# A windowed attention and ReGLU kernel: order of the first loads, weights 4 to 7 in one request, inverse sums ahead of the outputs

## The chip, the cores and the metric

One core of a Trainium2 chip. The time is device microseconds of one execution, with medians of several runs; the kernel before takes 266.7 us. A run counts as slow when it is over 1.5% above the fastest of its kernel. Two runs told here do, one of four in each of two experiments, which say so; the medians include them, the ratios don't. Kernels of different rounds are compared by their ratios. By the 2% mark that the prediction uses, a ratio between 0.98 and 1.02 would be called the same; where such a ratio is called a gain or a loss here, its interval leaves out 1. A ratio is the mean time of one kernel's fast runs over that of the other's of the same rounds, with a 95% interval, so it is not quite the ratio of the medians quoted beside it. A profile is of one execution and counts from its first instruction; its span is about 2 us shorter than the time.

## The reference, cut to what matters

```python
B, H, S, D = 4, 8, 768, 64                  # q, k, v: float32
scores = (q @ k.T) / 8                      # per head
keep   = (key < 4) | (0 <= query - key < 128)
a      = softmax(where(keep, scores, -1e9))
x      = concat_heads(a @ v)                # [3072, 512]
out    = (relu(x @ w_gate) * (x @ w_val)) @ w_out     # d_ff = 1536
```

Only a band of 128 keys and four sink keys counts. The work is cut in units of a batch and a pair of heads (four pairs a batch), and each unit in two parts of 384 queries. The FFN of a batch has two parts of 12 slots: a slot is 128 of the 1,536 columns, so it needs all four pairs' outputs of its part and one slice of each of the gate and value weights ("weights 0" to "weights 11").

## The kernel before

A static program: instructions are recorded in a fixed order, each engine runs its own in that order. Scores go through an exponential into `ee`. An output (called V below: V01 is pair 0, part 1) is two groups of matmuls, then work on DVE:

```python
PP = [pspool.tile([128, 2, 512], F32, name=f"pp{i}") for i in range(2)]   # two banks in each tile
G  = [pspool.tile([128, 512], F32, name=f"g{i}") for i in range(4)]       # one bank in each tile

def two():
    if head[0]:                              # the first 20 us
        srot[0] += 2
        return G[srot[0] % 4][:], G[(srot[0] + 1) % 4][:]
    x = pair()                               # the next of the two PP tiles
    return x[:, 0, :], x[:, 1, :]

def V(u, part, between=None):
    pv, pd = two()
    ...
    sums(pd, lambda j, h: ones[:])           # PE: row sums of ee
    if between: between()
    sums(pv, lambda j, h: vn[u.b % 2][:, j, 2 * u.p + h, :])   # PE: ee times V
    ...
    nc.vector.transpose(out=t1[:], in_=pd[:, 0:CUT])           # DVE: inverse of the row sums
    nc.vector.reciprocal(r[:], ...)
    nc.vector.transpose(out=R[:]..., in_=r[:]...)
    nc.vector.tensor_tensor(xT[...], pv[:, 0:CUT], R[:], op=Alu.mult)
```

There are 32 such outputs: four in the head (part 0 of the first batch), 28 among the FFN slots. V01 to V31 of the first batch follow slots 6 to 9. Loads in float32, nearly all on SP's queue: k and q of the first batch in eight halves, V in blocks j. Weights are requested by POOL, which casts them to bf16 on the way. POOL also casts most of k, q and V, in program order. A "gate" is a tiny write into a load's target that keeps SP from issuing the load before the program has come that far.

```python
# head, cut: loads and the requests of weights
for c in (6, 7):
    gate_half(c)                             # POOL
    load_half(c)
load_w(2, 4)
T_half(4); V(U[3], 0)
load_w(4, 6)
...
# what POOL and SP do ahead of an FFN slot
prep[0] += [("half", 6), ("lv0",), ("w", 6, 8), ("half", 7), ("w", 8, 10)]   # lv0: gate (POOL) and load of V, j 3 to 6
prep[2] += [("v", 0, j) for j in (3, 4, 5, 6)]                               # casts of V
prep[3] += [("w", 10, 12)]
prep[7] += [("load", 4), ("load", 5), ("load", 6), ("lv", 1)]                # next batch
```

The softmax here doesn't subtract the row's maximum and nothing guards it: scores larger than these inputs give would overflow.

Of the kernel before, what the change touches and what calls it, by code (L numbers as in the profile page):

```python
# [19 lines left out]
def kernel(  # L20
# [12 lines left out]
    nc = tc.nc  # L33
    B, H, S, D = q.shape
    assert (B, H, S, D) == (4, 8, 768, 64)
    NP = H // 2
# [46 lines left out]
           3: (1, 0, 152, [(252, 244, 0, 140), (380, 372, 140, 152)]),  # L83
           4: (1, 152, 507, [(252, 384, 152, 267), (380, 384, 267, 507)])}

    V2 = [(4, 2, 0, 255, 112), (5, 2, 255, 399, 240), (6, 2, 399, 419, 364)]
    VSEG = [[(0, 0, 0, 247, 0), (1, 0, 247, 499, 120), (2, 1, 0, 140, 244), (3, 1, 255, 267, 372)],
            [(2, 1, 140, 255, 0), (3, 1, 267, 507, 0)] + V2]
    VSEG0 = [[(0, 0, 0, 247, 0), (1, 0, 247, 499, 120), (2, 1, 0, 140, 244), (3, 1, 140, 152, 372)],
             [(2, 1, 152, 267, 0), (3, 1, 267, 507, 0)] + V2]  # L90

    class Unit:
        def __init__(self, i):
# [18 lines left out]
    def cast_half(c, copies=(nc.gpsimd.tensor_copy, nc.gpsimd.tensor_copy)):  # L112
        for src, dst, copy in ((kf, kn, copies[0]), (qf, qn, copies[1])):
            copy(half(dst, c).rearrange("p (n h d) -> p h n d", n=3, h=2),
                                  half(src, c).rearrange("p (h n d) -> p h n d", n=3, h=2))
# [16 lines left out]
    def cast_v(b, j, rows=128, copy=nc.gpsimd.tensor_copy):  # L132
        flat = lambda ap: ap.rearrange("p h d -> p (h d)")
        copy(flat(vn[b % 2][0:rows, j, :, :]), flat(vf[0:rows, j, :, :]))  # L134
# [86 lines left out]
    def two():  # L221
        if head[0]:
            srot[0] += 2
            return G[srot[0] % 4][:], G[(srot[0] + 1) % 4][:]
        x = pair()
        return x[:, 0, :], x[:, 1, :]

    def spin(n, bank=0):

        for _ in range(n):  # L230
            nc.tensor.matmul(out=G[bank][:], lhsT=idle[:, 0:128], rhs=idle[:], start=True, stop=True)
# [18 lines left out]

    def T_half(c):
        t, x = c % NP, c // NP
        if c <= NP:
            both = pair()
            tk, tq = both[:, 0, :], both[:, 1, :]
        else:
            tk, tq = G[3][:, 0:256], G[3][:, 256:512]
        for src, ps in ((kn, tk), (qn, tq)):
            for n in range(3):
                nc.tensor.transpose(ps.bitcast(BF16)[:, 128 * n:128 * n + 128], half(src, c)[:, 128 * n:128 * n + 128],  # L260
                                    ident[:])
        vk, vq = (ps.bitcast(BF16)[:, 0:HALF].rearrange("d (n p) -> d p n", p=128) for ps in (tk, tq))
        e = kE[t]

        for r0, r1, c0 in ((0, 40, 0), (40, 124, 128), (124, 128, 384)) if x == 0 else ((0, 80, 396), (80, 128, 640)):
            nc.scalar.copy(e[:, c0:c0 + 3 * (r1 - r0)].rearrange("d (p n) -> d p n", n=3), vk[:, r0:r1])
        (nc.scalar.copy if c in (2, 3, 4) else nc.vector.tensor_copy)(
            qT[t][:, x * HALF:x * HALF + HALF].rearrange("d (p n) -> d p n", n=3), vq)
        if x == 0:
            sinks(U[t], nc.scalar.copy)  # L270
# [20 lines left out]

    ready = {}

    def V(u, part, between=None):
        pv, pd = two()
        segs = (VSEG if u.b else VSEG0)[part]

        def sums(out, w):
            for i, (j, g, c0, c1, o0) in enumerate(segs):
                for h in range(2):  # L300
                    nc.tensor.matmul(out=out[64 * h:64 * h + 64, o0:o0 + c1 - c0], lhsT=w(j, h),  # L301
                                     rhs=ee[u.i % NE][:, g, h, c0:c1], start=i == 0, stop=i == len(segs) - 1,
                                     skip_group_check=True)

        sums(pd, lambda j, h: ones[:])
        if between:
            between()
        sums(pv, lambda j, h: vn[u.b % 2][:, j, 2 * u.p + h, :])
        t1 = npool.tile([128, CUT], F32, name="t1")
        R = npool.tile([128, CUT], F32, name="R")  # L310
        r = npool.tile([128, CUT // 32], F32, name="r")
        nc.vector.transpose(out=t1[:], in_=pd[:, 0:CUT])  # L312
        nc.vector.reciprocal(r[:], t1[:].rearrange("p (c e) -> p c e", e=32)[:, :, 0])
        nc.vector.transpose(out=R[:].rearrange("p (c e) -> p c e", e=32),  # L314
                            in_=r[:].unsqueeze(2).to_broadcast([128, CUT // 32, 32]))
        nc.vector.tensor_tensor(xT[u.b % 2][:, u.p, CUT * part:CUT * part + CUT], pv[:, 0:CUT], R[:], op=Alu.mult)  # L316
        ready[u.b, u.p, part] = True

    gvn = [0]

# [34 lines left out]
    with tc.manual_schedule():  # L355
# [11 lines left out]
        setup()  # L367
        cast_half(0)
        T_half(0)
        spin(5)  # L370
        cast_half(1)
        T_half(1)
        setup2()
        Sg(U[0], 0)
        Sg(U[0], 3)
        cast_v(0, 0)
        spin(2)
        Sg(U[1], 0)
        cast_v(0, 3, 16, nc.vector.tensor_copy)
        cast_half(2)  # L380
        cast_v(0, 1)
        cast_v(0, 2)
        Sg(U[1], 3)
        V(U[0], 0, lambda: T_half(2))
        cast_half(3, (nc.gpsimd.tensor_copy, nc.scalar.copy))
        Sg(U[2], 0)
        load_w(0, 2)
        V(U[1], 0)
        Sg(U[2], 3)
        T_half(3)  # L390
        cast_half(4)
# [1 line left out]
        Sg(U[3], 0)  # L393
        cast_half(5)
        Sg(U[3], 3)
        for c in (6, 7):
            gate_half(c)
            load_half(c)
        load_w(2, 4)
        T_half(4)  # L400
        V(U[3], 0)
        load_w(4, 6)
        Sg(U[0], 4)
        T_half(5)
        Sg(U[0], 2)
        spin(3, 2)
        head[0] = False


# [8 lines left out]
            at[st] = s  # L418
            plan[s].append(st)

        for s, w in {0: "S14 S12", 2: "H2", 3: "S24 S22 H3", 5: "S34 S32", 6: "V01", 7: "V11", 8: "V21",
                     9: "V31"}.items():
            for y in w.split():
                put(s, y, 0)
        for s, w in {11: "T0", 12: "T1", 13: "S00 S01", 14: "S10 S11", 15: "T2", 16: "S20 S21", 17: "V00", 18: "V10",
                     19: "T3", 20: "V20", 21: "S30 S31", 22: "V30 S02"}.items():
            for y in w.split():
                put(s, y, 1)
        for b in range(2, B + 1):
# [5 lines left out]
            for x, y in enumerate(w.split()):  # L435
                put(24 * (b - 1) + x // 2 * 2, y[0] + y[2:], b - (y[1] == "p"))
        prep = [[] for _ in slots]
        prep[0] += [("half", 6), ("lv0",), ("w", 6, 8), ("half", 7), ("w", 8, 10)]
        prep[2] += [("v", 0, j) for j in (3, 4, 5, 6)]
        prep[3] += [("w", 10, 12)]  # L440
        prep[7] += [("load", 4), ("load", 5), ("load", 6), ("lv", 1)]
        prep[9] += [("kq", 4)]
        prep[10] += [("load", 7), ("kq", 5)]
        prep[13] += [("kq", 6)]
        prep[14] += [("v", 1, j) for j in range(7)]
        prep[16] += [("kq", 7), ("td", 8), ("wo",)]
        for i in range(ND, len(U)):
            t = at["S", i - NP, 2] + 1
# [12 lines left out]
        for s, (b, g, m) in enumerate(slots):  # L461
            for x in prep[s]:
                if x[0] == "kq":
                    cast_kq(U[x[1]])
                elif x[0] == "load":
                    gate(U[x[1]])
                    load_kq(U[x[1]])
                elif x[0] == "half":
                    cast_half(x[1])
                elif x[0] == "w":  # L470
                    load_w(*x[1:])
                elif x[0] == "wo":
                    for c in range(3):
                        load_wo(c)
                elif x[0] == "td":
                    to_dram(U[x[1]])
                elif x[0] == "turn":
                    turn(U[x[1]])
                elif x[0] == "sinks":
                    sinks(U[x[1]], nc.gpsimd.tensor_copy)  # L480
                elif x[0] == "lv0":
                    for j in (3, 4, 5, 6):
                        nc.gpsimd.memset(vf[32:33, j, 0, 0:2], 0.0)
                        load_v(0, j, 16 if j == 3 else 0)
                elif x[0] == "lv":
                    for j in range(7):
                        load_v(x[1], j)
                else:
                    cast_v(*x[1:])
            chunk(b, g, m)  # L490
            for what, i, x in plan[s]:
                if what == "T":
                    T(U[i])
                elif what == "H":
                    T_half(NP + i)
                elif what == "S":
                    Sg(U[i], x)
                else:
                    V(U[i], x)
            for _ in range(3):  # L500
                if f2:
                    f2.popleft()()
            if s == 23:
                f2 += [lambda t=t, mm=mm: ffn2(0, t, mm) for t in range(6) for mm in range(FM)]
            if b > 0 and m == FM - 1:
                f2 += [lambda b=b, t=t, mm=mm: ffn2(b, t, mm) for t in range(3 * g, 3 * g + 3) for mm in range(FM)]
# [38 lines left out]
```

## Time and profile before

| | before |
|---|---|
| time, median | 266.7 us |
| span of the profiled run, mean granted PE clock | 264.3 us, 0.986 |
| PE busy, idle | 249.9 us, 14.4 us |
| FFN slot 0, slot 7, slot 24 start | 20.5, 39.2, 78.2 us |

The first lines to read are those that the prediction shows: PE is busy 95% of the span, its one large hole is at V01, and that hole is a wait for V. In a timeline: start, duration, engine, line, operation, in square brackets the idle time before it and what ended it. Here is what an output looks like where nothing disturbs it, in the timeline of PE and DVE of the kernel before (start, duration, engine, line, operation, in square brackets the idle time before it and what ended it):

```profile
95.07 0.53 PE L301 MATMUL pp<-ee,ones 128*64 128x115 bf16 x10
95.46 0.51 PE L301 MATMUL pp<-ee,vn 128*64 128x115 bf16 x10
95.90 0.39 PE L282 MATMUL pp<-qT,kE 64*128 64x247 bf16 x4
96.02 0.58 DVE L312 STREAM_TRANSPOSE t<-pp 128x384 f32<-128x384 f32 x1 [0.21 <-PE pp L301]
```

Both groups of sums follow each other without a gap, 95.07 to 95.90 = 0.83 us, and DVE's transpose starts after the second.

### The profile page before, as it was taken

How to read it: one execution, taken by the hardware profiler on the slowest of the kernel's cores; microseconds unless marked ns; L12 is line 12 of the kernel's file. 1: busy time of each engine (PE TensorE's matmuls, PEld its weight loads, DVE VectorE, ACT ScalarE, POOL GpSimd, SP SyncE). 2: the span in 40 equal slices, each digit the busy share in tenths (PEclk: the TensorE clock that was granted, in tenths of full speed). 3: DMA queues.
4: the chain of work that ended last, by engine and by line, in shares of the span. 5: the costliest groups of instructions: out<-in, count | busy, mean ns of one | idle time of the engine just before them, and what ended most of it. 6: DMA issues, size and time to landing. Idle time of an engine off the chain costs nothing.

```text
span 264.3 us, 5502 instructions
## 1 busy us (share of the span) xinstructions
PE 249.9 (95%) x2145; PEld 140.6 (53%) x2145; DVE 149.1 (56%) x314; ACT 117.4 (44%) x226; POOL 74.0 (28%) x106
## 2 busy tenths in 40 slices
PE   7889939998989999999999999999999999999994
PEld 3465515655646555555555555555555655555441
DVE  5577718777986774666537667657355642322000
ACT  3777802386353535553434355464344233332211
POOL 6687135299920014694000044000000000000000
PEclk9999968999999999999999999999999999999999
DMA  7999999939999259499412395310110111001232
GB/s 191 255 192 215 189 300 278 190 120 71 191 169 140 56 134 198 97 166 160 93 46 62 61 218 112 93 40 2 40 42 0 42 40 41 28 16 40 79 122 79
DMA packets 81266, 30.45 MB, mean 115 GB/s; under 512 B 65368, under 2 KB 77144, under 8 KB 81240
## 3 DMA queue, kind: packets, MB, share of 16 engines
q1 hardware_dynamic: 47944, 21.83, 33.3%
q0 software_dynamic: 32752, 7.87, 31.8%
q8 instruction: 17, 0.28, 0.5%
q10 hardware_dynamic: 544, 0.39, 0.5%
q14 instruction: 9, 0.07, 0.1%
HBM read 28.48 MB, written 9.44 MB: 143 GB/s over the span
## 4 chain that ended last, share of the span: by engine, by line
PE 77%; DMA 9%; DVE 4%; POOL 3%; issue 2%; SPq 2%; ACT 2%; ACTq 0%; POOLq 0%; DVEq 0%
PE g L348 21%; PE g L328 21%; PE g L333 20%; PE pp L301 7%; DMA vf<-in_v_dram 6%; PE pp L348 4%; PE pp L282 4%; DMA qf<-in_q_dram 4%; SPq L130 2%; DVE hT L335 1%; PE pp L240 1%; POOL vn L134 1%; DVE qT L248 1%; ACT ee L286 1%; DVE R L314 1%
## 5 line engine op out<-in xcount | busy, mean ns | idle before, releaser
L335 DVE TENSOR_TENSOR hT<-gs,g 128x384 bf16<-128x384 f32 x96 | 52.9, 551 | 64.9 <-PE g L333 63.1
L331 ACT ACTIVATE gs<-g 128x384 f32<-128x384 f32 x96 | 47.4, 494 | 76.9 <-PE g L328 75.7
L333 PE MATMUL g<-xT,wv 128*128 128x384 bf16 x384 | 78.8, 328 | 1.0 <-ACT ee L286 0.6
L328 PE MATMUL g<-xT,wg 128*128 128x384 bf16 x384 | 79.0, 328 | 0.0
L348 PE MATMUL g<-wo,hT 128*128 128x512 bf16 x240 | 64.1, 380 | 0.0
L286 ACT ACTIVATE ee<-pp 128x998 bf16<-128x998 f32 (+4 forms) x52 | 45.7, 903 | 31.3 <-PE pp L282 31.0
L328 PEld LDWEIGHTS <-wg 128*128 128x128 bf16 x384 | 36.1, 98 | 31.7 <-issue 1.2
L333 PEld LDWEIGHTS <-wv 128*128 128x128 bf16 x384 | 37.5, 98 | 27.1 <-DMA wv<-in_moe_w_val_dram 2.1
L348 PEld LDWEIGHTS <-hT 128*128 128x128 bf16 x288 | 26.2, 98 | 26.2 <-issue 2.1
L289 DVE TENSOR_TENSOR ee<-ee,msk 128x838 bf16<-128x838 bf16 (+4 forms) x48 | 29.3, 619 | 8.8 <-ACT ee L286 8.6
L134 POOL CAST vn<-vf 128x512 bf16<-128x512 f32 x28 | 17.8, 653 | 39.6 <-DMA vf<-in_v_dram 39.6
L151 POOL DMA_DIRECT2D qd<-in_q_dram x8 | 25.1, 4248 | 0.0
L151 POOL DMA_DIRECT2D kd<-in_k_dram x8 | 22.7, 3676 | 0.3 <-issue 0.3
L312 DVE STREAM_TRANSPOSE t<-pp 128x384 f32<-128x384 f32 x28 | 16.3, 581 | 8.9 <-PE pp L301 8.3
L352 ACT COPY ot<-g 128x512 f32<-128x512 f32 x20 | 11.7, 585 | 18.2 <-PE g L348 17.4
L282 PE MATMUL pp<-qT,kE 64*128 64x255 bf16 (+6 forms) x240 | 17.4, 246 | 2.0 <-DVE qT L248 1.0
L314 DVE STREAM_TRANSPOSE R<-r 128x384 f32<-128x384 f32 x32 | 18.5, 578 | 1.1
L301 PE MATMUL pp<-ee,vn 128*64 128x115 bf16 (+8 forms) x256 | 14.5, 236 | 4.2 <-POOL vn L134 4.2
L301 PEld LDWEIGHTS <-ones 128*64 128x64 bf16 x288 | 12.3, 110 | 9.7 <-issue 9.4
L316 DVE TENSOR_TENSOR xT<-pp,R 128x384 bf16<-128x384 f32 x28 | 15.6, 557 | 1.0
L301 PEld LDWEIGHTS <-vn 128*64 128x64 bf16 x288 | 12.5, 111 | 5.5 <-POOL vn L134 5.4
L301 PE MATMUL pp<-ee,ones 128*64 128x115 bf16 (+8 forms) x256 | 14.5, 239 | 0.1
(76 smaller groups left out, 126.7 us busy)
## 6 DMA issues: line engine op xcount, KB each, us to landing
out_dram<-ot SPq DMA_DIRECT2D x24, 256.0 KB
vf<-in_v_dram SPq DMA_DIRECT2D x12, 256.0 KB
vf<-in_v_dram SPq DMA_DIRECT2D x12, 224.0 KB
kf<-in_k_dram SPq DMA_DIRECT2D x8, 192.0 KB
wg<-in_moe_w_gate_dram POOLq DMA_DIRECT2D x6, 256.0 KB, 7.2
wv<-in_moe_w_val_dram POOLq DMA_DIRECT2D x6, 256.0 KB, 8.9
kf<-in_k_dram SPq DMA_DIRECT2D x4, 384.0 KB
qf<-in_q_dram SPq DMA_DIRECT2D x4, 384.0 KB
```

What stands on the lines that cost most here:

```text
L134: copy(flat(vn[b % 2][0:rows, j, :, :]), flat(vf[0:rows, j, :, :]))
L151: nc.gpsimd.dma_start(out=dst[u.i - ND].rearrange("s (h d) -> s h d", h=2), in_=x[u.b, 2 * u.p:2 * u.p + 2].rearrange("h s d -> s h d"))
L282: nc.tensor.matmul(out=ps[:, h, c0:c1], lhsT=kE[t][64 * h:64 * h + 64, x0:x0 + 128], rhs=qT[t][64 * h:64 * h + 64, q0:q0 + c1 - c0], start ...
L286: nc.scalar.activation(x, ps[:, :, b0:n], Act.Exp, bias=0.0, scale=scale)
L289: nc.vector.tensor_tensor(x, x, msk[:, g, m0:m0 + c1 - c0].unsqueeze(1).to_broadcast([128, 2, c1 - c0]), op=Alu.mult)
L301: nc.tensor.matmul(out=out[64 * h:64 * h + 64, o0:o0 + c1 - c0], lhsT=w(j, h), rhs=ee[u.i % NE][:, g, h, c0:c1], start=i == 0, stop=i == l ...
L314: nc.vector.transpose(out=R[:].rearrange("p (c e) -> p c e", e=32), in_=r[:].unsqueeze(2).to_broadcast([128, CUT // 32, 32]))
L328: nc.tensor.matmul(out=gp[:, 0:CUT], lhsT=wg[:, ko, m * 128:(m + 1) * 128], rhs=x[:, ko, c], start=ko == 0, stop=ko == KO - 1)
L331: nc.scalar.activation(gs[:], gp[:, 0:CUT], Act.Relu, bias=0.0, scale=1.0)
L333: nc.tensor.matmul(out=vp[:, 0:CUT], lhsT=wv[:, ko, m * 128:(m + 1) * 128], rhs=x[:, ko, c], start=ko == 0, stop=ko == KO - 1)
L335: nc.vector.tensor_tensor(h[:, m, c], gs[:], vp[:, 0:CUT], op=Alu.mult)
L348: nc.tensor.matmul(out=op, lhsT=hT[b % 2][:, m, t * 128:(t + 1) * 128], rhs=wo[:, m, :], start=m == 0, stop=m == FM - 1)
```

## The change

The intent: bring the loads of the first phase into PE's order of use, save a request, and start DVE's inverse sums of pairs 0 and 1 before PE forms their V sums. The diff, cut to its core (a rename of one table and the later slot for the casts of the next batch's V are left out):

```diff
 def T_half(c):
-        if c <= NP:
+        if c < 2:
+            tk, tq = two()
+        elif c <= NP:

-    def V(u, part, between=None):
-        pv, pd = two()
-        ...
-        sums(pd, lambda j, h: ones[:])
-        if between:
-            between()
-        sums(pv, lambda j, h: vn[u.b % 2][:, j, 2 * u.p + h, :])
+    def V1(u, part):
+        pv, pd = two()
+        sums(u, part, pd, lambda j, h: ones[:])
         t1 = ...; R = ...; r = ...
         nc.vector.transpose(out=t1[:], in_=pd[:, 0:CUT])
         nc.vector.reciprocal(...)
         nc.vector.transpose(out=R[:]...)
+        return u, part, pv, R
+
+    def V2(u, part, pv, R):
+        sums(u, part, pv, lambda j, h: vn[u.b % 2][:, j, 2 * u.p + h, :])
         nc.vector.tensor_tensor(xT[...], pv[:, 0:CUT], R[:], op=Alu.mult)
+
+    def V(u, part):
+        V2(*V1(u, part))

 # head: V1 of pairs 0 and 1 early, V2 of both later; V(U[3], 0) ahead of T_half(4); fewer spins
+        load_w(2, 4)
         for c in (6, 7):
             gate_half(c)
             load_half(c)
-        load_w(2, 4)
 ...
-        load_w(4, 6)
+        load_w(4, 8)

-        {0: "S14 S12", 2: "H2", 3: "S24 S22 H3", 5: "S34 S32", 6: "V01", ...}
+        {0: "S14 S12", 1: "H2", 2: "S24 S22 H3", 3: "S34 S32", 6: "V01", ...}
-        {11: "T0", 12: "T1", 13: "S00 S01", ..., 18: "V10", 19: "T3", ...}
+        {12: "T0", 13: "T1", 14: "S00 S01", ..., 19: "V10 T3", ...}
-        prep[0] += [("half", 6), ("lv0",), ("w", 6, 8), ("half", 7), ("w", 8, 10)]
-        prep[2] += [("v", 0, j) for j in (3, 4, 5, 6)]
-        prep[3] += [("w", 10, 12)]
-        prep[7] += [("load", 4), ("load", 5), ("load", 6), ("lv", 1)]
+        prep[0] += [("half", 6), ("half", 7), ("w", 8, 10), ("w", 10, 12)]
+        prep[3] += [("lv0",)]
+        prep[4] += [("v", 0, j) for j in (3, 4, 5, 6)]
+        prep[8] += [("load", 4), ("load", 5), ("load", 6), ("lv", 1)]
                 # in lv0
-                        nc.gpsimd.memset(vf[32:33, j, 0, 0:2], 0.0)
+                        nc.scalar.copy(vf[32:33, j, 0, 0:2], warm[32:33, :])
```

More of the change, by code (lines that the diff above doesn't have):

```diff
@@ L84 @@
            4: (1, 152, 507, [(252, 384, 152, 267), (380, 384, 267, 507)])}
-    V2 = [(4, 2, 0, 255, 112), (5, 2, 255, 399, 240), (6, 2, 399, 419, 364)]
+    VLAST = [(4, 2, 0, 255, 112), (5, 2, 255, 399, 240), (6, 2, 399, 419, 364)]
     VSEG = [[(0, 0, 0, 247, 0), (1, 0, 247, 499, 120), (2, 1, 0, 140, 244), (3, 1, 255, 267, 372)],
-            [(2, 1, 140, 255, 0), (3, 1, 267, 507, 0)] + V2]
+            [(2, 1, 140, 255, 0), (3, 1, 267, 507, 0)] + VLAST]
     VSEG0 = [[(0, 0, 0, 247, 0), (1, 0, 247, 499, 120), (2, 1, 0, 140, 244), (3, 1, 140, 152, 372)],
-             [(2, 1, 152, 267, 0), (3, 1, 267, 507, 0)] + V2]
+             [(2, 1, 152, 267, 0), (3, 1, 267, 507, 0)] + VLAST]
     class Unit:
@@ L292, with sums @@
     ready = {}
-    def V(u, part, between=None):
-        pv, pd = two()
-        segs = (VSEG if u.b else VSEG0)[part]
-        def sums(out, w):
-            for i, (j, g, c0, c1, o0) in enumerate(segs):
-                for h in range(2):
-                    nc.tensor.matmul(out=out[64 * h:64 * h + 64, o0:o0 + c1 - c0], lhsT=w(j, h),
-                                     rhs=ee[u.i % NE][:, g, h, c0:c1], start=i == 0, stop=i == len(segs) - 1,
-                                     skip_group_check=True)
-        sums(pd, lambda j, h: ones[:])
-        if between:
-            between()
-        sums(pv, lambda j, h: vn[u.b % 2][:, j, 2 * u.p + h, :])
+    def sums(u, part, out, w):
+        segs = (VSEG if u.b else VSEG0)[part]
+        for i, (j, g, c0, c1, o0) in enumerate(segs):
+            for h in range(2):
+                nc.tensor.matmul(out=out[64 * h:64 * h + 64, o0:o0 + c1 - c0], lhsT=w(j, h),
+                                 rhs=ee[u.i % NE][:, g, h, c0:c1], start=i == 0, stop=i == len(segs) - 1,
+                                 skip_group_check=True)
+    def V1(u, part):
+        pv, pd = two()
+        sums(u, part, pd, lambda j, h: ones[:])
         t1 = npool.tile([128, CUT], F32, name="t1")
@@ L369 @@
         T_half(0)
-        spin(5)
-        cast_half(1)
-        T_half(1)
+        spin(4, 1)
         setup2()
@@ L375 @@
         Sg(U[0], 3)
+        cast_half(1)
+        T_half(1)
         cast_v(0, 0)
-        spin(2)
+        cast_v(0, 3, 16, nc.vector.tensor_copy)
+        v0 = V1(U[0], 0)
         Sg(U[1], 0)
-        cast_v(0, 3, 16, nc.vector.tensor_copy)
         cast_half(2)
@@ L383 @@
         Sg(U[1], 3)
-        V(U[0], 0, lambda: T_half(2))
+        T_half(2)
+        v1 = V1(U[1], 0)
+        V2(*v0)
+        V2(*v1)
         cast_half(3, (nc.gpsimd.tensor_copy, nc.scalar.copy))
@@ L387 @@
         load_w(0, 2)
-        V(U[1], 0)
         Sg(U[2], 3)
@@ L398 @@
             load_half(c)
-        load_w(2, 4)
+        V(U[3], 0)
         T_half(4)
-        V(U[3], 0)
-        load_w(4, 6)
+        load_w(4, 8)
         Sg(U[0], 4)
@@ L405 @@
         Sg(U[0], 2)
-        spin(3, 2)
+        spin(2, 2)
         head[0] = False
@@ L419, in put @@
             plan[s].append(st)
-        for s, w in {0: "S14 S12", 2: "H2", 3: "S24 S22 H3", 5: "S34 S32", 6: "V01", 7: "V11", 8: "V21",
+        for s, w in {0: "S14 S12", 1: "H2", 2: "S24 S22 H3", 3: "S34 S32", 6: "V01", 7: "V11", 8: "V21",
                      9: "V31"}.items():
@@ L424 @@
                 put(s, y, 0)
-        for s, w in {11: "T0", 12: "T1", 13: "S00 S01", 14: "S10 S11", 15: "T2", 16: "S20 S21", 17: "V00", 18: "V10",
-                     19: "T3", 20: "V20", 21: "S30 S31", 22: "V30 S02"}.items():
+        for s, w in {12: "T0", 13: "T1", 14: "S00 S01", 15: "S10 S11", 16: "T2", 17: "S20 S21", 18: "V00",
+                     19: "V10 T3", 20: "V20", 21: "S30 S31", 22: "V30 S02"}.items():
             for y in w.split():
@@ L444 @@
         prep[13] += [("kq", 6)]
-        prep[14] += [("v", 1, j) for j in range(7)]
+        prep[15] += [("v", 1, j) for j in range(7)]
         prep[16] += [("kq", 7), ("td", 8), ("wo",)]
```

## The prediction

> **What bounds the kernel now.** I read the page first (busy shares, the chain of waits), then the PE timeline of the first 70 us with the idle time in front of each group, then POOL's timeline and the DMA queues by stretch, because a change of load order can only act where PE waits for a load.
>
> ```profile
> PE 249.9 (95%) x2145; PEld 140.6 (53%) x2145; DVE 149.1 (56%) x314; ACT 117.4 (44%) x226; POOL 74.0 (28%) x106
> PE 77%; DMA 9%; DVE 4%; POOL 3%; issue 2%; SPq 2%; ACT 2%; ACTq 0%; POOLq 0%; DVEq 0%
> ```
>
> PE is busy for 249.9 of 264.3 us, so all its idle time is 14.4 us, and the 9% of DMA in the chain is the part that a load order could touch. The page names it: loads of V and q. From 77 us on the chain is PE alone; what is won or lost before that is carried to the end unchanged. The timeline of PE shows where the one large hole lies:
>
> ```profile
> 33.72 0.33 PE L301 MATMUL pp<-ee,vn 128*64 128x115 bf16 x4
> 35.43 0.43 PE L301 MATMUL pp<-ee,vn 128*64 128x255 bf16 x2 [1.39 <-POOL vn L134]
> 38.45 0.33 PE L301 MATMUL pp<-ee,vn 128*64 128x144 bf16 x2 [2.59 <-POOL vn L134]
> 39.01 0.23 PE L301 MATMUL pp<-ee,vn 128*64 128x20 bf16 x2 [0.23 <-POOL vn L134]
> 39.17 1.46 PE L328 MATMUL g<-xT,wg 128*128 128x384 bf16 x4
> 42.76 0.82 PE L328 MATMUL g<-xT,wg 128*128 128x384 bf16 x4
> ```
>
> This is the second half of pair 0's output sum (V01, placed after FFN slot 6): 1.39 + 2.59 + 0.23 = 4.2 us of waiting for casts of V. The next slot then runs at half clock: it takes 39.17 to 41.84 = 2.67 us, where slot 8 takes 42.76 to 44.16 = 1.40 us; 1.3 us more. So this hole is worth about 5.5 us. POOL's casts wait in turn for the V loads:
>
> ```profile
> 30.59 0.61 POOL L134 CAST vn<-vf 128x512 bf16<-128x512 f32 x1 [3.92 <-DMA vf<-in_v_dram]
> 34.76 0.61 POOL L134 CAST vn<-vf 128x512 bf16<-128x512 f32 x1 [3.56 <-DMA vf<-in_v_dram]
> 37.78 1.17 POOL L134 CAST vn<-vf 128x512 bf16<-128x512 f32 x2 [2.41 <-DMA vf<-in_v_dram]
> ```
>
> SP issued these loads from 22.44 us, and the last landed at 37.7. Why 15 us? The stretches (time, then busy time of PE, PEld, DVE, ACT, POOL, clock, DMA share, GB/s) and the queues between 30 and 34 us answer:
>
> ```profile
> 24.00:26.00 2.00, 1.70 (x15) 0.99 (x14) 1.19 (x3) 0.70 (x3) 2.00 (x4) 1.00 1.45 200
> 26.00:30.00 4.00, 4.00 (x37) 2.46 (x36) 2.88 (x7) 3.35 (x8) 0.67 (x1) 1.00 1.35 200
> 30.00:34.00 4.00, 3.37 (x37) 1.71 (x35) 2.87 (x7) 2.63 (x7) 0.61 (x1) 1.00 1.35 183
> q0 software_dynamic: 993, 0.49, 89.4%
> q1 hardware_dynamic: 956, 0.24, 45.4%
> ```
>
> The DMA engines are full (share above 1), and weights (q0, packets of 512 B) and V (q1, 256 B) go through one for one: 993 packets against 956. V therefore gets only 0.24 MB of the 0.73 MB moved in 4 us. What sets the end of the stall is the sum of all that is queued before or beside V.
>
> **What the Trainium skill says.** "DMA: Bandwidth & Descriptors", section "Queues, rings and completion order", has each DMA engine take turns between the queue rows it has work for, packet by packet; the 993 to 956 above agrees. The same page, "Issuing engines are not separate DMA queues", says that loads issued from different engines end on the same 16 engines; the trace agrees, as V does not move faster for being on SP's queue. "TensorE: Matmul & The Clock Gate", section "The HAM clock gate", says that an idle window of about 3.4 us halves the PE clock; the trace agrees: granted clock 0.50 between 36 and 42 us, 2.67 us against 1.40 us. "Perfetto Trace Analysis", section "DMA Optimizations", says that larger transfers use the bandwidth better; here I doubt that it pays: the output weights come in rows of 1,024 B and move at 199 GB/s (68 to 70 us), rows of 512 B at 200 GB/s (24 to 26 us).
>
> **The change part by part.**
>
> *1. Loads.* Before, POOL requests weights 0-1 at 12.3 us, opens the gate of the last k/q halves at 15.8, requests 2-3 and 4-5 by 18.8, opens the gate of V at 22.4, requests 6-7 at 22.4 and 8-9 at 25.2; 10-11 only after the casts of V, at 38.9. After, 2-3 come ahead of the gate (k/q about 1.5 us later), 4-7 follow in one pair of requests of twice the size, then the casts of the last halves, then 8-9 and 10-11. The gate of V moves from POOL, slot 0, to ACT, slot 3, behind the copies of the last half: those need that half's load (landed about 24 us, now about 25.5), two casts of 0.5 and a transpose with copies of about 1 us, so V is requested at about 27.5 instead of 22.4 us.
>
> Now the sum. DMA is full from 12 us until V has landed, in both kernels: the weights 4-11 cover the stretch until V starts. In front of or beside V the new order has one more pair of requests, weights 10-11: 2 x 256 KB = 0.52 MB, at 200 GB/s 2.6 us. V (224 + 256 + 256 + 40 = 776 KB) is served one for one, so it is still the last to finish. Against it: less time is shared. At 183 GB/s shared, 122 of weights and 61 of V, I estimate 12% loss against each alone (weights 200; V alone about 240). V shares about 10 us now, about 6 then: 0.5 us back. Last V landing: 37.7 + 2.6 - 0.5 = 39.8 us. Then, as now, two casts (1.2 us) and the last sums (0.4 us): slot 7 starts at about 41.3, not 39.2 us. That is +2.1 us. The stall begins a little earlier or later, but that does not matter: its end is set by the load.
>
> *2. Head.* Two separate banks for the first transposes let DVE copy q while ACT copies k: the copy at 5.99 waited for ACT, some 0.6 us. The first scores come that much sooner, two fewer filler matmuls with a larger gap follow, and sums and inverses of pairs 0 and 1 (transposes of 0.58, reciprocal 0.23, 0.58) leave before their outputs need V. Pair 3's output comes before the transposes of half 4, which then delay the first FFN slot. I estimate slot 0 at 20.2 to 21.2 us against 20.5. Whatever the sign, nothing of it reaches the end: PE then waits for V anyway. Net 0.
>
> *3. Slots.* Half 2's transposes and the scores S24 to S32 come one or two slots earlier; same work, all before V01. Net 0. They may remove the 0.30 and 0.63 us waits ahead of slot 6, hidden by the same wait.
>
> *4. Second batch one slot later* (T0 11 to 12 and so on). The spacing stays, so its waits of 0.35 (55 us), 0.67 (62 us) and 0.73 us (74 us) mostly stay; perhaps 0.5 us goes, as V10 and T3 share a slot now. Its k/q loads are gated on ACT behind slot 7's activation, so at about 43 instead of 33 us; 2.3 MB at 400 GB/s take 6 us, landing by 50, and the transposes want them from 53. It fits.
>
> Sum: +2.1 - 0.5 = +1.6 us, 266.74 to about 268.3 us.
>
> **The rivals.** (a) *The change works as named*: with weights 4-7 through earlier and fewer shared rounds, V lands sooner and the 5.5 us hole closes. This would give 261 to 264 us. Against it: V is asked for 5 us later, with 0.52 MB more ahead and full engines. (b) *SP's issue becomes the bound.* V's 256 B packets on a free queue are not always quick: 113 GB/s at DMA share 0.50 between 48 and 50 us, while SP is issuing V of the next batch. If V's tail runs at that rate rather than 240, its last 0.45 MB takes 4 instead of 1.9 us: 270 to 271 us. (c) *A new wait later*: k/q, V and output weights of the next batch all start later behind a later V; if they miss their slots at 53, 66 and 83 us, each costs one or two us: 270 to 273 us. For it: POOL is busy 20.3 of the 24 us from 54 to 78. (d) *The head sets it*: only if V landed before 33 us.
>
> **Range and chances.** V's extra wait can be 0.5 (packets well overlapped) to 4 us (rival b), the later gain 0 to 1.5: 80% from 265.3 to 270.8 us. Faster by 2% (below 261.4) needs nearly the whole hole gone: 0.05. Slower by 2% (above 272.1) needs rivals b and c together: 0.09. Within: 0.86.
>
> **What would show it.** Right: casts of V ending at 40 to 42 us with the wait on the V load; V01's wait longer than 4.2 us, near 6 to 8; slot 7 again at half clock; weight requests 8-11 all issued before 30 us; PE from slot 8 on as before, shifted by about 2 us. Step 2 right: the q copy of the first half at about 5.4, and slot 0 near 20.5 with no effect at slot 7. Wrong: V landed by 36 us, a V01 wait below 4 us, or new waits of PE between 50 and 80 us; a slot order that reaches V01 later would also prove my "net 0" false.

## The result

| | before | after |
|---|---|---|
| time, median | 266.67 us | 302.46 us |
| ratio, 95% interval | | 1.134 (1.129 to 1.139) |
| span, mean granted PE clock | 264.3 us, 0.986 | 301.1 us, 0.971 |
| PE busy, idle | 249.9, 14.4 us | 257.7, 43.4 us |
| FFN slot 0, slot 7 start | 20.5, 39.2 us | 23.0, 44.5 us |

The kernel is 36 us slower, not 1.6. At slot 7 it is only 5.4 us behind, so most of the loss comes later, where the prediction saw nothing but PE at full work. Busy engines and the chain of waits of the changed kernel:

```profile
PE 257.7 (86%) x2116; PEld 145.9 (48%) x2141; DVE 153.0 (51%) x314; ACT 118.0 (39%) x230; POOL 71.3 (24%) x100
PE 72%; DVE 10%; DMA 7%; ACT 3%; issue 3%; POOL 2%; SPq 0%; DVEq 0%; POOLq 0%; ACTq 0%
```

DVE has gone from 4% to 10% of the chain although it has the same 314 instructions. (Of PE's 29 missing instructions, four are filler matmuls that the change leaves out; 25 are records that the trace lost, which makes PE's idle time look about 1 us too long.) The list of who waited for whom (total us, how often, the longest) names it. These are the lines of PE among the sums:

```profile
PE pp L300 <- DVE t L311: 24.8, 28, 1.9
PE pp L300 <- POOL vn L134: 5.8, 4, 4.1
```

The first line does not exist in the kernel before. In each of the 28 outputs outside the head PE now waits for DVE's transpose between its two groups of sums. One of them, from the timeline of the changed kernel, to be held against the four lines shown of before:

```profile
92.34 0.53 PE L300 MATMUL pp<-ee,ones 128*64 128x115 bf16 x10
92.99 0.58 DVE L311 STREAM_TRANSPOSE t<-pp 128x384 f32<-128x384 f32 x1
93.60 0.23 DVE L312 RECIPROCAL r<-t 128x12 f32<-128x12 f32 x1
93.62 0.54 PE L300 MATMUL pp<-ee,vn 128*64 128x115 bf16 x10 [0.74 <-DVE t L311]
94.09 0.36 PE L284 MATMUL pp<-qT,kE 64*128 64x255 bf16 x6
```

The transpose reads the row sums between 92.99 and 93.57, and the V sums start 0.05 us after it has ended, though they need nothing of it. From the first sum to the next work PE takes 94.09 - 92.34 = 1.75 us in place of 0.83.

The other part of the loss is there too, at V01. Timelines of PE and POOL of the changed kernel, for the lines of before that the prediction shows:

```profile
37.30 0.24 PE L300 MATMUL pp<-ee,vn 128*64 128x115 bf16 x2 [0.74 <-DVE t L311]
38.66 0.29 PE L300 MATMUL pp<-ee,vn 128*64 128x240 bf16 x2 [1.12 <-POOL vn L134]
43.03 0.43 PE L300 MATMUL pp<-ee,vn 128*64 128x255 bf16 x2 [4.08 <-POOL vn L134]
44.54 1.46 PE L334 MATMUL g<-xT,wg 128*128 128x384 bf16 x4
...
37.99 0.61 POOL L134 CAST vn<-vf 128x512 bf16<-128x512 f32 x1 [5.14 <-DMA vf<-in_v_dram]
43.16 1.17 POOL L134 CAST vn<-vf 128x512 bf16<-128x512 f32 x2 [0.18 <-DMA vf<-in_v_dram]
```

V's last casts end at 44.3 us; before it was 38.95, and I had predicted 40 to 42.

### The profile page after: what moved, and what is told of

It reads as the page before. It is cut to its first block, busy times and chain, and to the rows that moved or that the text cites. A ratio compares the mean times of both kernels' runs of the same rounds, so it can differ in the third digit from the quotient of the medians.

```text
span 301.1 us, 5493 instructions
## 1 busy us (share of the span) xinstructions
PE 257.7 (86%) x2116; PEld 145.9 (48%) x2141; DVE 153.0 (51%) x314; ACT 118.0 (39%) x230; POOL 71.3 (24%) x100
## 4 chain that ended last, share of the span: by engine, by line
PE 72%; DVE 10%; DMA 7%; ACT 3%; issue 3%; POOL 2%; SPq 0%; DVEq 0%; POOLq 0%; ACTq 0%
PE g L334 20%; PE g L339 19%; PE g L354 18%; PE pp L300 5%; DVE t L311 5%; DVE hT L341 4%; PE pp L284 4%; DMA qf<-in_q_dram 4%; PE pp L354 3%; DMA vf<-in_v_dram 3%; ACT ee L288 2%; PE pp L240 1%; DMA kf<-in_k_dram 1%; DVE qT L248 1%; PE g L231 1%
## 5 line engine op out<-in xcount | busy, mean ns | idle before, releaser
L334 PE MATMUL g<-xT,wg 128*128 128x384 bf16 x384 | 80.8, 334 | 0.4 <-DVE qT L269 0.2
L339 PE MATMUL g<-xT,wv 128*128 128x384 bf16 x384 | 79.7, 331 | 0.0
L354 PE MATMUL g<-wo,hT 128*128 128x512 bf16 x217 | 61.5, 386 | 1.3 <-issue 0.3
L334 PEld LDWEIGHTS <-wg 128*128 128x128 bf16 x384 | 36.8, 100 | 33.3 <-issue 3.8
L339 PEld LDWEIGHTS <-wv 128*128 128x128 bf16 x384 | 38.2, 100 | 26.1 <-issue 2.0
L300 PE MATMUL pp<-ee,vn 128*64 128x115 bf16 (+8 forms) x256 | 15.4, 239 | 30.6 <-DVE t L311 24.8
L300 PEld LDWEIGHTS <-vn 128*64 128x64 bf16 x288 | 15.6, 110 | 33.3 <-issue 26.7
L134 POOL CAST vn<-vf 128x512 bf16<-128x512 f32 x28 | 16.8, 617 | 39.8 <-DMA vf<-in_v_dram 39.8
L284 PE MATMUL pp<-qT,kE 64*128 64x255 bf16 (+6 forms) x240 | 17.5, 249 | 2.0 <-ACT qT L269 1.0
L300 PEld LDWEIGHTS <-ones 128*64 128x64 bf16 x288 | 12.8, 111 | 11.3 <-issue 10.7
```

The costliest lines, as they stand in the source:

```text
L284: nc.tensor.matmul(out=ps[:, h, c0:c1], lhsT=kE[t][64 * h:64 * h + 64, x0:x0 + 128], rhs=qT[t][64 * h:64 * h + 64, q0:q0 + c1 - c0], start ...
L300: nc.tensor.matmul(out=out[64 * h:64 * h + 64, o0:o0 + c1 - c0], lhsT=w(j, h), rhs=ee[u.i % NE][:, g, h, c0:c1], start=i == 0, stop=i == l ...
L334: nc.tensor.matmul(out=gp[:, 0:CUT], lhsT=wg[:, ko, m * 128:(m + 1) * 128], rhs=x[:, ko, c], start=ko == 0, stop=ko == KO - 1)
L339: nc.tensor.matmul(out=vp[:, 0:CUT], lhsT=wv[:, ko, m * 128:(m + 1) * 128], rhs=x[:, ko, c], start=ko == 0, stop=ko == KO - 1)
L354: nc.tensor.matmul(out=op, lhsT=hT[b % 2][:, m, t * 128:(t + 1) * 128], rhs=wo[:, m, :], start=m == 0, stop=m == FM - 1)
```

## The experiments

Two theories. **Recording order:** `pv` and `pd` are the two halves of one PP tile. With DVE's read of `pd` recorded between PE's two writes, the program makes the second write wait for the read, as it would if it tracks reads and writes by the tile and not by its halves. **Loads (rival):** the new load order is the cause, through a V that lands late and a DMA traffic that gets in the way later; the waits on DVE only fill time that PE would lose anyway.

### The old recording order put back into the changed kernel

```diff
 def V(u, part):
-    V2(*V1(u, part))
+    pv, pd = two()
+    sums(u, part, pd, ...)
+    sums(u, part, pv, ...)
+    # then DVE's transpose, reciprocal, transpose and product
```

> The changed kernel with one thing put back: outside the head, both sums of an output (ones, then V) are recorded before DVE's transpose of the ones sum, as in the kernel before. Theory (order of recording: DVE's read of one half of the shared PSUM tile now stands between PE's two writes to it, so PE waits for it 28 times): the waits of the V sums on DVE's transpose (24.8 us in 28) go, and what is left is the 5.4 us that the changed kernel had lost by FFN slot 7: 270 to 274 us. Rival (the new load order and later V are the cause, and the waits only fill time that PE would wait anyway): 295 to 303 us.

Measured: 273.36 us, 1.029 (1.023 to 1.035). No wait of PE on the transpose is left in the list. Against the kernel before in the same rounds (265.81 us) it is 7.5 us slower, where the changed kernel was 35.8 us slower in its own (302.46 - 266.67). So about 28.2 us of the 35.8 hang on the order in which these instructions are recorded, and 7.5 us do not.

### The new recording order alone in the kernel before

```diff
     sums(pd, lambda j, h: ones[:])
     if between: between()
-    sums(pv, ...)
     # DVE's transpose, reciprocal, transpose
+    sums(pv, ...)
     # DVE's product
```

> The kernel before with one thing changed: DVE's transpose, reciprocal and transpose are recorded between the ones sum and the V sum in every output. Theory (order of recording): about 0.9 us more for each of the 28 outputs outside the head and some throttled windows: 291 to 298 us, with PE waiting on the transpose about 25 us in 28. Rival (load order): stays at 266 to 269 us.

Measured: 296.72 us, 1.113 (1.106 to 1.120), with loads and head as before (one of the four runs, 298.51 us, is slow). The line in its list of waits, and its busy times:

```profile
PE pp L301 <- DVE t L311: 24.8, 28, 1.9
PE 257.3 (87%) x2145; PEld 144.9 (49%) x2145; DVE 152.3 (52%) x314; ACT 117.3 (40%) x226; POOL 73.5 (25%) x106
```

The span grows by 294.8 - 264.3 = 30.5 us: PE's idle time by 23.1 (37.5 in place of 14.4), its busy time by 7.4 (257.3 in place of 249.9). For the latter the clock answers in part: a mean of 0.976 of 294.8 us is 14.2 us at half speed (twice 0.024 times 294.8), a mean of 0.986 of 264.3 us is 7.4 us; 6.8 us more at half speed cost up to 3.4 us of work. The lines already shown give an estimate for the other 4 us: in the kernel before, the two groups of sums overlap by 0.14 us (95.07 + 0.53 against 95.46); with a wait between them they do not overlap, and 28 times 0.14 is 3.9 us. The rival falls for the large part of the loss. This part and the loads alone (1.0225, below) add up: 11.3% and 2.2% are 13.5%, and the changed kernel is 13.4% slower.

### Is it the shared tile?

The order of recording could make PE wait for another reason than the tile. In the changed kernel, with its order, the row sums of eight outputs (slots 6 to 9 and 18 to 22) go to a G tile that is free there:

```diff
 def V1(u, part):
     pv, pd = two()
+    if not head[0] and at_slot[0] < 23:
+        pd = G[3][:]
```

> The changed kernel, with the order of recording kept, but in the eight outputs of FFN slots 6 to 9 and 18 to 22 the ones sum goes to a bank of its own tile instead of the other half of the same tile. Theory (the wait comes from the shared tile): these eight lose their wait, the other 20 keep it: the total wait on the transpose falls from 24.8 to about 15 to 17 us and the time by 5 to 10 us, to 292 to 298 us. Rival (the order alone makes PE wait, whatever the tile): no change, 300 to 303 us.

Measured: 294.44 us, 1.103 (1.099 to 1.107), about 8 us less than the changed kernel (1.134 less 1.103 of 266 us); one of the four runs, 297.17 us, is slow. List of waits and one of the eight outputs in the timeline:

```profile
PE pp L301 <- DVE t L314: 17.5, 20, 1.9
...
75.73 0.48 PE L301 MATMUL g<-ee,ones 128*64 128x247 bf16 x8
76.06 0.46 PE L301 MATMUL pp<-ee,vn 128*64 128x247 bf16 x8
```

20 waits are left of 28, and the eight without one are those with two tiles: their sums follow each other without a gap. The head of the changed kernel says the same, where `two()` gives two G tiles and no output waits. So the wait comes from the shared tile together with the order; neither alone makes it. The expectation of 15 to 17 us of waits was missed by half a microsecond: it took the eight waits for longer ones, but they were worth 7.3 us, little more than eight times the mean of 0.89 us.

### The loads, gates and slots alone

The kernel before with the diff's loads, gate on ACT, slots and preparation; head and recording order as before.

> The kernel before with only the loads, gates and slots of the change (weights 4 to 7 in one request and earlier, 8 to 11 ahead of V, gate of V on ACT in slot 3, slots moved); head and recording order as before. My prediction's sum for this part was +1.6 us (268.3). The changed kernel's trace has slot 7 at 44.5 instead of 39.2 us, of which slot 0 is already 2.5 late by the head: so I now expect 268 to 272 us, V's last cast near 43 us.

Measured: 271.64 us, 1.0225 (1.020 to 1.025). So the loads carry most of what the recording order does not. Slot 7 starts at 42.80 us, 3.6 late. My sum had said 2.1 and rested on full DMA engines. The stretches of this run (time, busy times of PE, PEld, DVE, ACT, POOL, clock, DMA share, GB/s) show that they were not:

```profile
26.00:28.00 2.00, 1.97 (x21) 1.07 (x19) 1.11 (x2) 1.47 (x4) 0.50 (x1) 1.00 1.18 225
28.00:30.00 2.00, 0.51 (x6) 0.38 (x7) 1.38 (x3) 1.21 (x3) 1.07 (x2) 1.00 0.26 45
30.00:32.00 2.00, 2.00 (x20) 1.16 (x19) 1.10 (x2) 1.94 (x8) 2.00 (x4) 1.00 0.56 57
32.00:34.00 2.00, 2.00 (x15) 1.21 (x13) 1.62 (x5) 1.67 (x4) 0.35 (x1) 1.00 1.37 185
```

From 28 to 32 us the engines move about 50 GB/s where they moved 225. All that was requested has landed, and the next requests hang on it: POOL asks for weights 8 to 11 only after it has cast the last k/q half, and ACT opens V's gate only after that half's copies. The changed kernel itself has the same gap: 87 GB/s from 28 to 30 us, 32 from 30 to 32. POOL's timeline of this run (DMA issues stand there as well):

```profile
16.94 0.74 POOL L167 DMA_DIRECT2D wg<-in_moe_w_gate_dram  x1
22.86 0.50 POOL L114 CAST kn<-kf 128x384 bf16<-128x384 f32 x1 [4.43 <-PE g L333]
26.89 0.50 POOL L114 CAST kn<-kf 128x384 bf16<-128x384 f32 x1 [1.33 <-DMA kf<-in_k_dram]
28.93 0.50 POOL L114 CAST qn<-qf 128x384 bf16<-128x384 f32 x1 [1.54 <-DMA qf<-in_q_dram]
29.39 0.74 POOL L167 DMA_DIRECT2D wg<-in_moe_w_gate_dram  x1
```

After slot 7 another 1.8 us are lost (the span is 5.4 longer). Slot 10 starts 4.6 us late (51.86 against 47.24, same work done): slots after a longer stall run longer at half clock, 1.0 us. And where V10 and T3 now share slot 19, T3's transposes wait 0.69 us for DVE; the prediction had seen half a microsecond of gain there.

### One request or two for weights 4 to 7

```diff
-        load_w(4, 8)
+        load_w(4, 6)
+        load_w(6, 8)
```

> The run with the loads alone, but weights 4 to 7 in two pairs of requests with rows of 512 B instead of one with rows of 1,024 B. Theory (queues take turns packet by packet, so rows of twice the size halve the share of the k/q halves, which land late, and POOL, which waits for them before it requests 8 to 11, leaves the DMA engines dry near 28 to 31 us): the last half's cast starts at 25.5 to 27 us instead of 28.9, the gap in the DMA traffic goes, slot 7 starts at about 40 to 41 us instead of 42.8, time 1.005 to 1.015 of before. Rival (the size of a request plays no part): 1.020 to 1.025 as in the loads alone.

Measured: 270.42 us, 1.0153 (1.013 to 1.018). The expectation holds in direction and misses in size: the last half's q cast starts at 27.11 instead of 28.93, slot 7 at 42.13, not 40 to 41, and the time is just above the range. The queues of the two runs, rows of 1,024 B (22 to 26 us), then of 512 B (19 to 24 us; packets, MB, share of 16 engines), q0 the weights, q1 the k/q halves:

```profile
q0 software_dynamic: 528, 0.52, 77.9%
q1 hardware_dynamic: 525, 0.38, 39.6%
```

```profile
q0 software_dynamic: 1117, 0.56, 86.1%
q1 hardware_dynamic: 743, 0.54, 40.2%
```

In the first the two queues are served packet for packet, 528 to 525, so rows of twice the size give weights 0.52 MB in 4 us and leave 0.38 to the halves; the weights are not needed yet, the halves are. In the second, which begins before the halves' packets do, the halves get nearly as many bytes as the weights. The fairest comparison is one stretch in which both queues are served in both runs, 23 to 25 us: with the larger rows 270 packets against 265, and 0.19 MB for the halves; with the smaller ones 386 against 388, and 0.28 MB. The dry stretch shrinks (137 GB/s between 28 and 32 us) and does not go, since V is still requested behind the last half, at 28.99 us. So the size of the request is a part of the loss, the smaller one.

### The requests of weights 8 to 11 ahead of the casts

```diff
-        prep[0] += [("half", 6), ("half", 7), ("w", 8, 10), ("w", 10, 12)]
+        prep[0] += [("w", 8, 10), ("w", 10, 12), ("half", 6), ("half", 7)]
```

> The run with the loads alone, but weights 8 to 11 are requested ahead of the casts of the last k/q halves, so that the DMA engines always have work. Theory (my prediction's sum holds when the engines never run dry: V lands 2.1 us later than in the kernel before): slot 7 at about 41 us instead of 42.8, time 1.008 to 1.016 of before. Rival (the late request of V itself is what counts, not the dry stretch): slot 7 at 42.5 us or later, 1.02 or more.

Measured: 268.40 us, 1.0076 (1.005 to 1.011), just under the range. The DMA engines now have work until V has landed, and slot 7 starts at 40.58, 1.4 us late, although V is requested later than in any other run (31.92 us). So in this run the late request of V cost nothing that shows, with the engines full, and the dry stretch of the run with the loads alone did. The stretch of the same time in this run:

```profile
28.00:32.00 4.00, 2.34 (x26) 1.39 (x24) 2.61 (x6) 2.59 (x9) 1.00 (x2) 1.00 1.39 201
```

In the profiled run PE waited 4.1 us in slots 1 to 3 for the casts of the last k/q halves and only 2.2 us, in four pieces, at V01; no single wait was over 1.7 us, and the clock was not halved there. It is the fastest of these runs (267.2 to 269.4 us), which is luck; so slot 7's 1.4 us rest on one favourable execution, and the time on four.

### The head alone

Kernel before with the diff's head, the loads in the old order.

> The kernel before with only the head of the change (separate banks for the first two transposes, sums and inverses of pairs 0 and 1 ahead of their V sums, pair 3's output ahead of the transposes of half 4, fewer filler matmuls); loads, slots and the recording order of all later outputs as before. My prediction: net 0 at the end (slot 0 may start at 20.2 to 21.2 us, and V is waited for anyway), so 265 to 267 us. Rival (head and loads add up: the changed kernel with the old order was 1.029, the loads alone 1.0225): slot 0 starts near 22 us, and some of it reaches the end: 267 to 268.5 us.

Measured: 266.03 us, 0.9988 (0.997 to 1.001). Slot 0 starts at 21.52 us, one microsecond late and just outside the predicted range. The rival falls: slot 0's time does not reach the end. V's last casts start at 37.50, slot 7 at 38.89. With the loads of the change it cannot be told apart whether the head costs something: 1.029 for both against 1.0225 for the loads alone, intervals 1.023 to 1.035 and 1.020 to 1.025; in the changed kernel slot 0 is 2.5 us late (PE waits for copies of half 4, and the clock is halved there).

### A better kernel

V01's stall is set by V's landing, so PE can do another slot first, and weights 10 and 11 can be asked for where POOL only waits for V. From the kernel before:

```diff
-        {..., 6: "V01", 7: "V11", 8: "V21", 9: "V31"}
+        {..., 7: "V01", 8: "V11", 9: "V21 V31"}
-        prep[2] += [("v", 0, j) for j in (3, 4, 5, 6)]
-        prep[3] += [("w", 10, 12)]
-        prep[7] += [("load", 4), ("load", 5), ("load", 6), ("lv", 1)]
-        prep[9] += [("kq", 4)]
+        prep[2] += [("v", 0, 3), ("v", 0, 4), ("w", 10, 12), ("v", 0, 5), ("v", 0, 6)]
+        prep[9] += [("load", 4), ("load", 5), ("load", 6), ("lv", 1), ("kq", 4)]
```

> A try for a better kernel, from the kernel before: the second halves of the outputs one slot later (slots 7, 8, 9, 9), so that PE has slot 6 to do while V lands; weights 10 and 11 requested between two casts of V and ahead of the next batch's loads, which go to slot 9. Theory (V's landing sets the end of the stall; PE can fill 1.4 us of it): the stall shrinks from 4.2 to about 2.8 us, slot 12 two us earlier, 263.5 to 265.5 us. Rival (the DMA traffic or DVE, with two outputs in slot 9, takes its place): 266 us or more.

Measured: 263.98 us, 0.990 (0.986 to 0.994), better than both kernels. The stall at V01 in this run's timeline, to be held against 1.39, 2.59 and 0.23 of before:

```profile
37.29 0.26 PE L301 MATMUL pp<-ee,vn 128*64 128x144 bf16 x2 [1.76 <-POOL vn L134]
37.84 0.20 PE L301 MATMUL pp<-ee,vn 128*64 128x20 bf16 x2 [0.30 <-POOL vn L134]
```

2.1 us of waits are left of 4.2, better than the 2.8 expected, and slot 12 starts at 48.89 instead of 51.04. Not all is gained: PE now waits 0.99 us for weights in slot 6, where it had waited 0.63 us for ACT, and 0.36 us for DVE ahead of slot 12. The two parts of this edit, the later outputs and the moved requests, were not run apart, so what each is worth stays open.

The same with the change's head added:

> The better kernel of the run before (second halves of the outputs a slot later, weights 10 and 11 between two casts of V) with the head of the change added. Theory (the head's part is worth nothing, as V's landing comes after it): the same as without it, 263 to 265.5 us, 0.985 to 0.995 of before. Rival (with the stall shortened to 2 us, the head's gain or loss shows): below 262.5 or above 266 us.

Measured: 263.97 us, 0.989 (0.987 to 0.992). The head adds nothing here either.

## Why the prediction was wrong

By its own steps:

- **Step 2 is the one that failed.** It says of the split "sums and inverses of pairs 0 and 1 leave before their outputs need V" and closes "Net 0". It took the split for a matter of the head. But the new `V` calls `V1` and then `V2` for every output, so in all 28 outputs of the slots DVE's transpose is recorded before PE's V sums, and these share the PP tile with the row sums. A term was missing from the sum: 28 waits of 0.89 us, 24.8 us, and what comes with them. Put back, it is worth about 28 us. Within such an output the order of PE's own instructions is the same in both; the difference is in the semaphore that the first V sum waits for.
- **Step 2, what it said of the head itself,** holds: 0.9988 alone. Its guess of slot 0 (20.2 to 21.2 us) does not hold: 21.5 us alone, 23.0 us in the changed kernel. The change leaves out four filler matmuls, not two (17 become 13).
- **Step 1 had the mechanism and a wrong premise.** V served packet for packet and last to finish, 0.52 MB more to move: with full engines this cost 1.4 us at slot 7 and 1.0076 in time (my sum of all steps was 1.6 us; measured 2.05). "DMA is full from 12 us until V has landed, in both kernels" was false: requests 8 to 11 and V both hang on the last k/q half, which the larger rows make late, and the engines moved about 50 GB/s for 4 us. That made it, in the run with the loads alone, 3.6 us at slot 7 and 5.8 in time. In the changed kernel that half's q had landed only at about 29.4 us, where the prediction had 25.5, so V was requested at 31.2 us, not 27.5. (The loss by sharing, put at 12%, comes out as 14% from its own figures, 122/200 + 61/240 = 0.86; this changes the sum by less than 0.1 us.)
- **Step 1 on the larger request.** I doubted that it pays, and rightly; that it takes bandwidth from what is needed first, the very turn-taking that I had cited, I did not draw.
- **Step 4** expected 0.5 us back from V10 and T3 in one slot; it cost 0.69 us.
- **Rivals.** (a), the hole closes, did not happen. (b), a slow tail of V, and (c), late loads of the next batch, are not needed to explain the time: the runs with old recording order show PE waiting for no load after V01 and before slot 24 that the kernel before does not wait for. None of the four named the recording order. "PE from slot 8 on as before" was named as a sign, and it was wrong at once in the trace; so was the premise that from 77 us on the chain is PE alone and carries what went before unchanged to the end.
- **The half clock.** The prediction set the 0.50 from 36 to 42 us beside an idle window of about 3.4 us. Its own trace has no such window before the clock falls: PE goes idle at 34.05 us, and the granted clock is 1.00 until 35.0 and 0.50 from 35.25 on, after some 1.2 us. The size, 1.3 us for slot 7, is read rightly; the condition is not shown.

## What to carry to other kernels

When a helper is split, look at every caller and at the waits, not only at the order on each engine: in this program a read by another engine recorded between two writes to one tile put a wait there, though the halves lie in different banks. Keep the two results in two tiles, or record both writes first. Where full DMA engines were the bound here, what counted was the sum of bytes ahead and that no request waited for an earlier one to land; and a request of larger rows took its share from its neighbours.

## What the Trainium skill lacked or had wrong

- "PSUM — Partial Sum Buffer", section "PSUM bank collisions raise a hardware error", lets two engines work on different banks at once. No page says that a program like this one can make them wait all the same when the two banks lie in one tile: 28 waits, 24.8 us; with eight of the outputs in two tiles, 20 waits, 17.5 us.
- "Perfetto Trace Analysis", section "DMA Optimizations", advises larger transfers. Here rows of 1,024 B in place of 512 B made the kernel slower (1.0225 against 1.0153), because queues that take turns by packet (528 to 525) give the larger packets more of the engines; no page draws this from the turn-taking.
- "TensorE: Matmul & The Clock Gate", section "The HAM clock gate", ties the half clock in its table to an idle window of about 3.4 us; a later section of the page knows that short pauses between groups of matmuls can do it too, but gives no figure for how short. In the kernel before, the clock fell some 1.2 us into PE's idle time (34.05 to 35.25 us). In the changed kernel's head it fell with no single wait over 1.01 us, after a stretch in which PE was busy for two thirds of the time (stretches as above; the clock is the third figure from the end):

```profile
18.00:20.00 2.00, 1.33 (x22) 1.09 (x22) 1.23 (x4) 0.90 (x4) 0.45 (x1) 1.00 1.38 185
20.00:22.00 2.00, 1.39 (x14) 0.89 (x15) 1.04 (x3) 1.48 (x4) 0.00 (x0) 0.68 1.08 190
22.00:24.00 2.00, 1.78 (x11) 0.80 (x9) 1.56 (x4) 1.17 (x3) 0.66 (x1) 0.50 1.14 220
```
